# First batch of a fused attention and feed-forward kernel: load pieces dealt over both hardware queues, sines of k moved to ScalarE, transposed-q copies issued later

## The chip, the cores and the metric

One core of one Trainium2 chip. The metric is the device time in microseconds (us) of one execution. A run here is one such execution; each comparison has several, taken on the same chip as runs of the kernel before. The profile is of one execution, and its span (344.9 us for the kernel before) is about 1.8 us shorter than the time of the same execution.

## The reference

Cosformer attention (linear attention with position weights), then a gated feed-forward block. Batch 8, 8 heads, 576 positions, head dimension 64; model width 512, inner width 1536.

```python
theta = pi / 2 * arange(S) / S
phi(x) = concat([max(x, 0) * cos(theta), max(x, 0) * sin(theta)])   # 64 -> 128 features
kv  = einsum('bhsf,bhsd->bhfd', phi(k), v);   z = sum_s phi(k)
num = phi(q) @ kv;   den = phi(q) . z + 1e-6
x   = num / den                               # to [4608, 512], heads side by side
out = (gelu(x @ w_gate) * (x @ w_val)) @ w_out
```

## The kernel before

The kernel is one hand-ordered stream per engine. Nearly all of its time is the feed-forward matmuls, which cannot start before the first 256 rows of `x` exist. The path to them, the head of the kernel, is what the change touches. In batch 0:

- q, k and v arrive in pieces by pairs of heads (`m` counts four pairs).
- VectorE or ScalarE forms the cosine and sine halves of phi in bf16 (`prep_wide` on VectorE, `prep_act` on ScalarE; "sines" below are the sine halves of k that `prep_act` makes); v is cast to bf16.
- TensorE transposes phi(q) into PSUM; ScalarE and VectorE copy it out (`turn_q_pe`).
- Dummy matmuls (`keep_warm`) bridge the wait; they are meant to have TensorE at its full clock when real work comes. In the profile of this kernel each of them takes 311 ns up to about 11.4 us and 219 ns from then on. That moment is called the release of the clock.
- `kv_unit(0, 2)` multiplies phi(k) by v in two groups of two pairs, with a ScalarE copy after each group. `nm_unit` then makes numerators and denominators, `xt_unit` the transposed `x`, and `gv_unit` the first gate and value matmuls.

```python
load(nc.sync, "qf", q, 0, ((0, 2), (2, 2)), 0, 4)       # pieces (first pair, pairs), rows j 0..4
load(nc.scalar, "kf", k, 0, ((0, 2), (2, 2)))
load(nc.sync, "vf", v, 0, ((0, 2), (2, 1), (3, 1)))
load(nc.sync, "qf", q, 0, ((0, NP),), 4, R)
# ... constants; sin and cos tables on ScalarE; Gelu table load ...

for m in range(NP):
    for part in range(2):
        prep_wide("qp", 0, 0, 4, m, part)               # VectorE, 8 scalings of q
prep_act("kp", 0, 1, 0, 2)                              # ScalarE, 9 sines of k, pairs 0-1
turn_q_pe(0, 0, 4, (0, 1))                              # PE transposes, then copies at once
prep_wide("kp", 0, 0, R, 0, 0)
prep_wide("kp", 0, 0, R, 1, 0)
for m in (2, 3):
    for part in range(2):
        prep_wide("kp", 0, 0, R, m, part)               # VectorE, cosines AND sines of pairs 2-3
cast_v(0, 0, 2, nc.scalar.copy)
cast_v(0, 2, 1, nc.vector.tensor_copy)
cast_v(0, 3, 1, nc.vector.tensor_copy)
keep_warm(60)
kv_unit(0, 2)
nm_unit(0, 0)
nm_unit(0, 1, 0)
keep_warm(8)
xt_unit(0, 0)
# ...

def kv_unit(b, groups=1):
    # ... PSUM view psv, result tile kv ...
    for g in range(groups):
        # ... 36 matmuls of two pairs (72 of four, if groups is 1) ...
        nc.scalar.copy(kv[:, g * per:(g + 1) * per], psv[:, g * per:(g + 1) * per])
```

## Time and profile before

| | before |
|---|---|
| median of 3 runs | 346.81 us (346.61 to 347.16) |
| span of the profiled execution | 344.9 us |
| first kv matmul | 13.40 us |
| first num/den matmul | 15.98 us |
| first gate matmul | 19.80 us |

From the page of the kernel before: busy time of each engine, and TensorE's busy tenths in 40 slices of 8.6 us. (PE is TensorE, PEld its weight loads, DVE VectorE, ACT ScalarE, POOL GpSimd.)

```profile
PE 324.1 (94%) x2702; PEld 180.5 (52%) x2740; DVE 193.3 (56%) x534; ACT 138.0 (40%) x273; POOL 30.2 (9%) x51
PE   2889998989899999999999999999999999999994
```

TensorE is close to full in every slice but the first two or three and the last. So the head is where a change to batch 0 can gain: at most some of the 19.8 us.

The chain of waits of the kernel before, in order of time (start us, length us, what):

```profile
1.26 5.49 DMA qf<-in_q_dram
6.77 1.44 DVE qp L153 x4
...
8.87 4.60 PE psum L403 x60
13.47 0.71 PE psum L243 x36
...
14.20 0.39 ACT kv_sb L250
...
15.98 0.43 PE psum L259 x8
```

L403 is keep-warm, L243 kv, L250 the copy of kv, L259 num/den. The second q piece holds VectorE until 6.77 us; 60 keep-warm matmuls run to 13.47; the kv matmuls of pairs 2-3 wait for the copy of pairs 0-1.

Some lines of the timeline of the same stretch (start us, length us, engine, line, operation, output<-input, shapes, count, and in brackets the idle time before it and what ended it):

```profile
5.55 2.73 ACT L167 ACTIVATE kp<-kf,sin_t 128x128 bf16<-128x128 f32 x9 [0.54 <-DMA kf<-in_k_dram]
8.91 0.42 DVE L209 COPY qT_178<-psum 128x512 bf16<-128x512 bf16 x1 [0.70 <-PE psum L202]
9.22 1.16 ACT L175 CAST vx_119<-vf 128x1152 bf16<-128x1152 f32 x1
9.58 2.09 DVE L153 SCALAR_TENSOR_TENSOR kp<-kf,cos_t 128x576 bf16<-128x576 f32 x3
13.59 1.41 DVE L175 CAST vx_119<-vf 128x576 bf16<-128x576 f32 x2
14.62 0.89 PE L243 MATMUL psum<-vx_119,kp 64*128 64x65 bf16 x36 [0.47 <-ACT kv_sb L250]
```

VectorE is the busy one: from 8.91 to 15.00 us it has no gap, and its last v cast is the last input of pairs 2-3. ScalarE is idle from 10.4 to 14.2 us. That idle time is what the change wants to use.

### The profile page before, as it was taken

Reading aid. Unit: us, or ns where it says so; the run is one execution under the profiler, and the core shown is the slowest. Engines: PE = TensorE matmul, PEld = TensorE weight load, DVE = VectorE, ACT = ScalarE, POOL = GpSimd, SP = SyncE. Lnnn points to the kernel's source line nnn. Section 1 sums busy time; section 2 is a strip of 40 time slices with the busy share of each in tenths; the row PEclk is TensorE's granted clock in tenths of the full one; section 3 lists DMA queues with packets and bytes.
Section 4 is the critical chain, followed back from the end, with each engine's and each line's share of the span. In section 5 each row is a group of like instructions: output and inputs, shape, how many; then the busy total and the mean of one; then the engine's idle time right before and its main releaser. Section 6 shows DMA issues by size and latency. Waiting matters only on the chain.

```text
span 344.9 us, 6823 instructions
## 1 busy us (share of the span) xinstructions
PE 324.1 (94%) x2702; PEld 180.5 (52%) x2740; DVE 193.3 (56%) x534; ACT 138.0 (40%) x273; POOL 30.2 (9%) x51
## 2 busy tenths in 40 slices
PE   2889998989899999999999999999999999999994
PEld 1878757755445554555455545554555444444443
DVE  3777765993792598258825883588345222322300
ACT  7257965533433343334323433343244333223221
POOL 1831022000200200020002000110000000000000
PEclk9999999999999999999999999999999999999999
DMA  7999985019659907990789079606811111211124
GB/s 278 263 272 303 244 276 185 2 30 357 226 76 212 349 6 102 227 343 3 98 190 381 6 86 208 244 0 79 153 30 33 30 30 36 52 36 30 32 61 92
DMA packets 47889, 48.81 MB, mean 142 GB/s; under 512 B 25201, under 2 KB 33137, under 8 KB 47857
## 3 DMA queue, kind: packets, MB, share of 16 engines
q1 hardware_dynamic: 38672, 35.27, 40.3%
q0 software_dynamic: 8480, 11.80, 14.4%
q10 hardware_dynamic: 704, 1.31, 1.1%
q8 instruction: 21, 0.34, 0.4%
q14 instruction: 12, 0.09, 0.1%
HBM read 37.75 MB, written 9.44 MB: 137 GB/s over the span
## 4 chain that ended last, share of the span: by engine, by line
PE 89%; DVE 5%; DMA 2%; ACT 2%; issue 1%; SPq 0%; DVEq 0%; ACTq 0%
PE psum L321 52%; PE psum L352 25%; PE psum L243 3%; PE psum L259 3%; PE psum L299 2%; DMA qf<-in_q_dram 2%; PE psum L202 1%; PE psum L403 1%; DVE kp L143 1%; DVE x_sb L272 1%; DVE hT L332 1%; PE psum L564 1%; ACT xT L306 0%; DVE qp L153 0%; ACT gel L329 0%
## 5 line engine op out<-in xcount | busy, mean ns | idle before, releaser
L332 DVE TENSOR_TENSOR hT<-gel,psum 128x512 bf16<-128x512 f32 (+4 forms) x132 | 77.5, 589 | 126.8 <-PE psum L321 115.1
L329 ACT ACTIVATE gel<-psum 128x512 f32<-128x512 f32 (+4 forms) x132 | 68.6, 520 | 127.6 <-PE psum L321 121.5
L321 PE MATMUL psum<-xT,wg_sb 128*128 128x512 bf16 (+4 forms) x515 | 113.6, 339 | 2.4 <-ACT xT L306 1.4
L321 PE MATMUL psum<-xT,wv_sb 128*128 128x512 bf16 (+4 forms) x516 | 113.1, 339 | 0.6
L352 PE MATMUL psum<-wo_sb,hT 128*128 128x512 bf16 x407 | 104.3, 379 | 1.2 <-issue 0.8
L321 PEld LDWEIGHTS <-wg_sb 128*128 128x128 bf16 x528 | 48.4, 98 | 47.2 <-issue 2.1
L321 PEld LDWEIGHTS <-wv_sb 128*128 128x128 bf16 x528 | 49.0, 98 | 45.4
L352 PEld LDWEIGHTS <-hT 128*128 128x128 bf16 x420 | 38.7, 98 | 39.0
L306 ACT COPY xT<-psum 128x512 bf16<-128x512 bf16 (+1 forms) x44 | 22.0, 509 | 24.4 <-PE psum L299 24.3
L361 ACT COPY o_sb<-psum 128x512 f32<-128x512 f32 x35 | 20.5, 586 | 27.7 <-PE psum L352 26.3
L272 DVE TENSOR_TENSOR x_sb<-psum,rec 128x512 bf16<-128x512 f32 x40 | 27.7, 691 | 1.4
L143 DVE TENSOR_SCALAR qp<-qf,cos_t 128x256 bf16<-128x256 f32 x68 | 24.0, 353 | 0.0
L143 DVE TENSOR_SCALAR kp<-kf,cos_t 128x256 bf16<-128x256 f32 x63 | 21.6, 347 | 0.0
L143 DVE TENSOR_SCALAR qp<-qf,sin_t 128x256 bf16<-128x256 f32 x59 | 20.4, 346 | 0.0
L143 DVE TENSOR_SCALAR kp<-kf,sin_t 128x256 bf16<-128x256 f32 x57 | 19.8, 347 | 0.0
L299 PE MATMUL psum<-ident,x_sb 128*128 128x128 bf16 x160 | 15.5, 219 | 1.7 <-DVE x_sb L272 1.5
L202 PE MATMUL psum<-ident,qp 128*128 128x128 bf16 x108 | 9.2, 232 | 7.4 <-DVE qp L153 6.3
L175 POOL CAST vx_121<-vf 128x576 bf16<-128x576 f32 x12 | 7.5, 672 | 96.3 <-DMA vf<-in_v_dram 96.3
L175 POOL CAST vx_119<-vf 128x576 bf16<-128x576 f32 (+1 forms) x10 | 7.3, 767 | 65.3 <-DMA vf<-in_v_dram 65.3
L243 PEld LDWEIGHTS <-kp 64*128 64x128 bf16 x576 | 10.1, 94 | 4.8 <-issue 2.6
L299 PEld LDWEIGHTS <-x_sb 128*128 128x128 bf16 x160 | 10.1, 97 | 4.7 <-DVE x_sb L272 3.5
L202 PEld LDWEIGHTS <-qp 128*128 128x128 bf16 x108 | 7.3, 103 | 9.4 <-DVE qp L153 7.2
(90 smaller groups left out, 161.1 us busy)
## 6 DMA issues: line engine op xcount, KB each, us to landing
out_dram<-o_sb SPq DMA_DIRECT2D x70, 128.0 KB, 2.4
qf<-in_q_dram SPq DMA_DIRECT2D x5, 1152.0 KB, 11.6
kf<-in_k_dram SPq DMA_DIRECT2D x5, 1152.0 KB, 6.0
vf<-in_v_dram SPq DMA_DIRECT2D x5, 1152.0 KB, 9.2
qf<-in_q_dram POOLq DMA_DIRECT2D x2, 1152.0 KB, 16.3
kf<-in_k_dram POOLq DMA_DIRECT2D x2, 1152.0 KB, 11.5
vf<-in_v_dram POOLq DMA_DIRECT2D x2, 1152.0 KB, 11.7
wo_sb<-in_moe_w_out_dram POOLq DMA_DIRECT2D x2, 768.0 KB, 17.8
```

Source lines behind the costliest of these rows:

```text
L143: nc.vector.tensor_scalar(dst[:, m:m + n, j, part * D:(part + 1) * D], src[:, m:m + n, j], 0.0, (cos_t, sin_t)[part][:, j:j + 1], op0=ALU.max,
L175: copy(vx_tiles[b % 2][:, m:m + n, :, 0:D], staged["vf", b][:, m:m + n].rearrange("p m (j d) -> p m j d", j=R),)
L202: nc.tensor.transpose(out=views[m // per][:, m % per, j], in_=phi["qp", b][:, m, j0 + j, :], identity=ident,)
L243: nc.tensor.matmul(psv[:, pair, i], lhsT=kp[rr, pair, j, :], rhs=vx[rr, pair, j, :], start=(j == 0), stop=(j == R - 1),)
L272: nc.vector.tensor_tensor(x, nm[:, :, :, 0:D], rec[:, :, :, None].to_broadcast([128, 2, 4, D]), op=ALU.mult,)
L299: nc.tensor.transpose(out=ps[:, ct, :], in_=x[:, ct * 128:(ct + 1) * 128], identity=ident)
L306: nc.scalar.copy(xT_block(blk)[:, :, c:c + m], ps[:, :, o:o + m])
L321: nc.tensor.matmul(ps[:, 0:n], lhsT=w[:, ct, js], rhs=xt[:, ct, cc:cc + n], start=(ct == 0), stop=(ct == CT - 1),)
L329: nc.scalar.activation(gel[:, 0:n], g_ps[:, 0:n], AF.Gelu)
L332: nc.vector.tensor_mul(hT[blk][:, jt, cc:cc + n], gel[:, 0:n], v_ps[:, 0:n])
L352: nc.tensor.matmul(o_ps[i], lhsT=hT[blk][:, jt, tt * 128:(tt + 1) * 128], rhs=wo_sb[:, jt, :], start=(jt == 0), stop=(jt == JT - 1),)
L361: nc.scalar.copy(o_sb, o_ps.pop(i))
```

## The change

Intent: let q arrive first on both queues, so that VectorE does all q scalings in one run; give the sines of pairs 2-3 to ScalarE; take the v cast of pairs 0-1 in exchange; put the copies of transposed q last, since num/den needs them only after kv. The loads of v pair 3 and of the rest of q go to ScalarE's queue. Keep-warm goes from 60 to 50, with 8 more after kv.

```diff
-    load(nc.sync, "qf", q, 0, ((0, 2), (2, 2)), 0, 4)
-    load(nc.scalar, "kf", k, 0, ((0, 2), (2, 2)))
-    load(nc.sync, "vf", v, 0, ((0, 2), (2, 1), (3, 1)))
-    load(nc.sync, "qf", q, 0, ((0, NP),), 4, R)
+    load(nc.sync, "qf", q, 0, ((0, 2),), 0, 4)
+    load(nc.scalar, "qf", q, 0, ((2, 2),), 0, 4)
+    load(nc.sync, "kf", k, 0, ((0, 2),))
+    load(nc.scalar, "kf", k, 0, ((2, 2),))
+    load(nc.sync, "vf", v, 0, ((0, 2),))
+    load(nc.sync, "vf", v, 0, ((2, 1),))
 ...  (after the sine and cosine tables on ScalarE)
+    load(nc.scalar, "vf", v, 0, ((3, 1),))
+    load(nc.scalar, "qf", q, 0, ((0, NP),), 4, R)
 ...  (turn_q_pe split: the transposes, and turn_copies for the copies)
+    turn_q_pe(0, 0, 4, (0, 1), (None, None))
     prep_act("kp", 0, 1, 0, 2)
-    turn_q_pe(0, 0, 4, (0, 1))
     prep_wide("kp", 0, 0, R, 0, 0)
     prep_wide("kp", 0, 0, R, 1, 0)
-    for m in (2, 3):
-        for part in range(2):
-            prep_wide("kp", 0, 0, R, m, part)
-    cast_v(0, 0, 2, nc.scalar.copy)
+    cast_v(0, 0, 2, nc.vector.tensor_copy)
+    prep_act("kp", 0, 1, 2, 2)
+    prep_wide("kp", 0, 0, R, 2, 0)
+    prep_wide("kp", 0, 0, R, 3, 0)
     cast_v(0, 2, 1, nc.vector.tensor_copy)
     cast_v(0, 3, 1, nc.vector.tensor_copy)
+    turn_copies(0, 0, 4, (0, 1), (nc.scalar.copy, nc.vector.tensor_copy))
 ...
-    keep_warm(60)
+    keep_warm(50)
     kv_unit(0, 2)
+    keep_warm(8)
     nm_unit(0, 0)
```

More of the change, by code (lines that the diff above doesn't have):

```diff
@@ L206, in turn_q_pe, with turn_copies @@
                 )
-        for g, copy in zip(range(len(banks)), engines):
+        if engines[0] is not None:
+            turn_copies(b, j0, n, banks, engines)
+    def turn_copies(b, j0, n, banks, engines):
+        per = NP // len(banks)
+        for g, copy in enumerate(engines):
+            ps = psum[:, banks[g]].bitcast(BF16)[:, 0:per * n * 128].rearrange(
+                "f (m j c) -> f m j c", m=per, j=n
+            )
             for i in range(2):
@@ L212, in turn_q_pe @@
                     ].rearrange("f m (j p) -> f m j p", p=64),
-                    views[g][:, :, :, i * 64:(i + 1) * 64],
+                    ps[:, :, :, i * 64:(i + 1) * 64],
                 )
```

## The prediction

> **What bounds the kernel now.** The busy table gives PE 94% of a 344.9 us span; the 40-slice row shows PE at 8-9 tenths everywhere after the first slice. From 19.80 us on (first gate matmul) PE is dense and nothing changes. What can be won is the head. The chain of waits reads there: q load to 6.77 us; four q scalings (1.44); transposes; 60 keep-warm matmuls, 8.87 to 13.47; kv matmuls of pairs 0-1; ScalarE copy; kv matmuls of pairs 2-3, 14.62 to 15.53; copy; first num/den matmul at 15.98; then 3.8 us (divide, transpose, xT copy) to 19.80. By the timeline, VectorE works without a break from 8.91 to 15.00: qT copies (0.75), six k scalings (0.67 apart), then the v casts that release pairs 2-3. So VectorE and the keep-warm run bind together.
>
> **What the change does.** Loads: the second q piece lands at 6.77 now, behind 2304-byte k packets of the other queue. I estimate the q pieces at 3.8 and 4.9, k at 6.5 and 7.8 (was 5.55 and 8.7), v of pairs 0-1 at 9.5 (about 9.0 now), from packet rates in the trace. The Trainium skill, "DMA: Bandwidth & Descriptors", section "Issuing engines are not separate DMA queues", says queues share the same 16 engines and only interleave. The trace agrees: both queues together move 391 to 396 GB/s from 4 to 10 us; order changes, not rate.
>
> VectorE: all q scalings in one run, 3.8 to 6.5 (ended 8.2). It loses two k scalings (2 x 0.67) to ScalarE and gains the 1152-column v cast (about 1.27). The qT copies move to last. The sum hardly changes; it starts earlier but, I expect, sits 1.5 us waiting for v after two k scalings (8.0 to 9.5). Then cast to 10.8, k to 12.1, casts to 13.5, qT copies to 14.25.
>
> ScalarE: 18 sines at 0.30: 6.6 to 12.0 (was 9 from 5.55), qT copies to 13.0, then the first kv copy; it loses the 1.16 us cast. Two DMA issues (1.1 us) push the Gelu table load, hidden behind k.
>
> PE: transposes end near 7.0 instead of 8.87; 50 keep-warm matmuls end near 11.5. "TensorE: Matmul & The Clock Gate", Part 1, makes the warm-up a time (about 3.4 us of activity), not a count; in the trace keep-warm durations fall from 311 to 219 ns at about 11.3 us. So fewer, earlier matmuls may run mostly cold. Kv of pairs 0-1 at 11.5, of pairs 2-3 at 13.45 to 14.3, copy to 14.7, num/den at 14.8.
>
> **On the path.** About 1.2 us of 15.98 is gained, and carried whole through the 3.8 us and the dense remainder, since weights are issued earlier too (their gate, the second k piece, lands 0.9 us sooner).
>
> **Prediction:** 345.6 us, 344.4 to 346.6. Faster by over 2%: 0.01; within 2%: 0.98; slower: 0.01.
>
> **What would show it.** First q scaling before 4.2 and last ending before 7; VectorE idle 1 to 2 us before the large v cast, released by the v load; first sine at 6.2 to 7; first num/den at 14.3 to 15.3; first gate matmul at 18.1 to 19.1; the interval from there to the end unchanged within 0.3 us.
>
> **What would make it wrong.** v landing near 8.5 would add up to 1 us of gain. v at 10.5, or sines plus qT copies holding the first kv copy beyond 13.5, would eat the gain; so would a clock still throttled at 12 us, or later stages re-absorbing the head start in a load wait.

## The result, and the profile after

| | before | after |
|---|---|---|
| median of 4 runs | 346.99 us (346.61 to 347.25) | 345.87 us (345.63 to 346.18) |
| span of the profiled execution | 344.9 | 344.4 |
| first num/den matmul | 15.98 | 15.47 |
| first gate matmul | 19.80 | 19.29 |
| from there to the end of the span | 325.1 | 325.1 |

The ratio is 0.9969, with a 95% interval of 0.9952 to 0.9987: a gain of 0.3%, real but within the 2% that counts as the same. A ratio is the mean time of one kernel's runs over that of the other's of the same rounds, so it is not quite the ratio of the medians. The profiles are 0.5 us apart and the medians 1.1, because a profile is of one execution: that of before took 346.72 us, less than its median, and that of the changed kernel 346.18, the slowest of its four. The changed kernel was profiled once more below: its gate matmul then came at 19.09.

The chain of waits of the changed kernel, which answers to that of before:

```profile
1.75 8.46 DMA vf<-in_v_dram
...
10.23 1.04 DVE vx_119 L180
11.27 1.32 DVE kp L158 x2
12.59 1.32 DVE vx_119 L180 x2
13.92 0.34 DVE qT_194 L222
14.26 0.75 PE psum L256 x36
...
```

Here L158 is VectorE's scalings, L172 the sines, L180 the v casts, L222 the copies of transposed q, L417 keep-warm, L256 kv and L263 the copy of kv.

Taken at its word, the chain says that the v load now binds, and behind it VectorE, down to its copy of transposed q. But the kv matmuls of pairs 2-3 (L256) don't read transposed q. Some lines of the timeline show another candidate:

```profile
4.34 0.42 DVE L158 SCALAR_TENSOR_TENSOR qp<-qf,cos_t 128x256 bf16<-128x256 f32 x1 [2.75 <-DMA qf<-in_q_dram]
7.57 4.88 PE L417 MATMUL psum<-ident 128*128 128x128 bf16 x50
7.60 5.38 ACT L172 ACTIVATE kp<-kf,sin_t 128x128 bf16<-128x128 f32 x18 [2.59 <-DMA kf<-in_k_dram]
10.23 1.04 DVE L180 CAST vx_119<-vf 128x1152 bf16<-128x1152 f32 x1 [1.26 <-DMA vf<-in_v_dram]
12.51 1.40 DVE L180 CAST vx_119<-vf 128x576 bf16<-128x576 f32 x2
12.88 0.57 ACT L222 COPY qT_194<-psum 128x512 bf16<-128x512 bf16 x1
13.35 0.58 ACT L222 COPY qT_195<-psum 128x512 bf16<-128x512 bf16 x1
13.82 0.37 ACT L263 CAST kv_sb<-psum 128x260 bf16<-128x260 f32 x1
13.84 0.41 DVE L222 COPY qT_194<-psum 128x512 bf16<-128x512 bf16 x1
14.25 0.75 PE L256 MATMUL psum<-vx_119,kp 64*128 64x65 bf16 x36 [1.11 <-DVE qT_194 L222]
```

ScalarE, half idle before, now works from 7.60 to 14.19 us without a gap: 18 sines, two q copies, and only then the copy of kv of pairs 0-1, which had been ready since 13.13 (12.38 plus 0.75). That copy ends at 14.19; the first VectorE q copy ends at 14.25; the matmuls start at 14.25. Two ends 0.06 us apart: the profile infers the releaser, and cannot be trusted between them.

### The profile page after: what moved, and what is told of

It reads as the page before. It is cut to its first block, busy times and chain, and to the rows that moved or that the text cites. A ratio compares the mean times of both kernels' runs of the same rounds, so it can differ in the third digit from the quotient of the medians.

```text
span 344.4 us, 6826 instructions
## 1 busy us (share of the span) xinstructions
PE 324.5 (94%) x2700; PEld 180.9 (53%) x2738; DVE 192.4 (56%) x533; ACT 139.3 (40%) x281; POOL 30.5 (9%) x51
## 4 chain that ended last, share of the span: by engine, by line
PE 88%; DVE 6%; DMA 2%; ACT 1%; issue 1%; SPq 0%; DVEq 0%; ACTq 0%
PE psum L334 52%; PE psum L365 25%; PE psum L256 3%; PE psum L272 3%; PE psum L312 2%; DMA vf<-in_v_dram 2%; DVE kp L148 1%; PE psum L207 1%; DVE x_sb L285 1%; DVE hT L345 1%; PE psum L579 1%; DVE vx_119 L180 1%; ACT xT L319 0%; DVE kp L158 0%; ACT gel L342 0%
## 5 line engine op out<-in xcount | busy, mean ns | idle before, releaser
L180 POOL CAST vx_121<-vf 128x576 bf16<-128x576 f32 x12 | 7.5, 669 | 96.0 <-DMA vf<-in_v_dram 65.1
L180 POOL CAST vx_119<-vf 128x576 bf16<-128x576 f32 (+1 forms) x10 | 7.2, 765 | 65.6 <-DMA vf<-in_v_dram 65.6
L256 PEld LDWEIGHTS <-kp 64*128 64x128 bf16 x576 | 10.1, 95 | 5.4 <-issue 3.4
## 6 DMA issues: line engine op xcount, KB each, us to landing
qf<-in_q_dram SPq DMA_DIRECT2D x5, 1152.0 KB, 11.6
kf<-in_k_dram POOLq DMA_DIRECT2D x2, 1152.0 KB, 11.4
vf<-in_v_dram POOLq DMA_DIRECT2D x2, 1152.0 KB, 11.8
```

The lines of the kernel that those rows point to most:

```text
L180: copy(vx_tiles[b % 2][:, m:m + n, :, 0:D], staged["vf", b][:, m:m + n].rearrange("p m (j d) -> p m j d", j=R),)
L256: nc.tensor.matmul(psv[:, pair, i], lhsT=kp[rr, pair, j, :], rhs=vx[rr, pair, j, :], start=(j == 0), stop=(j == R - 1),)
```

## The experiments

Two theories of what binds the head of the changed kernel:

- **A, ScalarE.** The first kv copy stands behind 18 sines and two q copies in ScalarE's queue, and it releases pairs 2-3.
- **B, the v load and VectorE**, as the chain of waits says.

And a question of the change itself: is it the load order or the compute order that gains? Each kernel got five to six runs, with 11 runs of the kernel before in the same set of four; all gave correct results. The three sets (rows 2 to 5, 6 to 9 and 10 to 13) ran on three different chips, so a difference between medians of two sets may hold a difference of the chips; the ratio, which is to runs of the kernel before on the same chip, is the safer figure. "First gate" is the first gate matmul in the kernel's profile.

| kernel | median us | ratio to before (95%) | first gate us |
|---|---|---|---|
| before, three sets | 346.92, 346.84, 347.10 | | 19.80 |
| changed, again | 345.91 | 0.9972 (0.9960 to 0.9985) | 19.09 |
| loads only | 345.75 | 0.9964 (0.9951 to 0.9977) | 18.98 |
| compute order only | 345.72 | 0.9973 (0.9955 to 0.9990) | 18.55 |
| changed, kv copy first | 345.19 | 0.9952 (0.9940 to 0.9964) | 18.28 |
| changed, k scalings before v cast | 346.04 | 0.9973 (0.9959 to 0.9986) | 19.18 |
| changed, 9 wide sines | 345.68 | 0.9960 (0.9948 to 0.9973) | 19.02 |
| before, 50 keep-warm | 346.68 | 0.9989 (0.9976 to 1.0002) | 19.86 |
| changed, three edits | 345.50 | 0.9955 (0.9942 to 0.9968) | 18.43 |
| changed, kv in one group | 345.46 | 0.9955 (0.9942 to 0.9968) | 18.39 |
| changed, k by single pairs | 345.27 | 0.9948 (0.9936 to 0.9960) | 18.61 |
| old loads, one group | 345.33 | 0.9950 (0.9935 to 0.9964) | 18.12 |
| new loads, one group | 344.43 | 0.9925 (0.9913 to 0.9938) | 17.52 |

In every one of these profiles the span less the time of the first gate matmul is 325.0 to 325.4 us. So whatever is gained or lost in the head goes whole into the span, and the first gate matmul can be read in place of the span.

### The changed kernel again (no edit)

> The changed kernel once more, unedited, as the control of this set: ratio to the kernel before 0.9955 to 0.9985, the first num/den matmul at 15.3 to 15.6 us and the first gate matmul at 19.1 to 19.4 us, as in its first profile (15.47 and 19.29; before 15.98 and 19.80). If the gain of 1.1 us by the medians is typical and the profiled 0.5 us was an unlucky execution, the first gate matmul is nearer 18.9.

It held, to within 0.03 us: 345.91 us and ratio 0.9972, first gate at 19.09 (19.1 or later expected), first num/den at 15.27 (15.3 or later). In this execution VectorE ended its casts sooner, and the profile names ScalarE for the same wait that it put down to VectorE before:

```profile
13.57 0.74 DVE L222 COPY qT<-psum 128x512 bf16<-128x512 bf16 x2
13.62 0.37 ACT L263 CAST kv_sb<-psum 128x260 bf16<-128x260 f32 x1
14.05 0.75 PE L256 MATMUL psum<-vx,kp 64*128 64x65 bf16 x36 [0.90 <-ACT kv_sb L263]
```

### The kv copy ahead of the q copies

```diff
-    turn_copies(0, 0, 4, (0, 1), (nc.scalar.copy, nc.vector.tensor_copy))
 ...
-    kv_unit(0, 2)
+    kv_unit(0, 2, lambda: turn_copies(   # called in kv_unit, after the copy of group 0
+        0, 0, 4, (0, 1), (nc.scalar.copy, nc.vector.tensor_copy)
+    ))
```

> The changed kernel with the four q copies issued after the first kv copy instead of before it. Theory A (ScalarE binds: 18 sines to 12.98, two q copies to 13.9, then the first kv copy, which releases the kv matmuls of pairs 2-3 at 14.25): these start at 13.5 to 13.6, the first num/den matmul at about 14.95 instead of 15.47, 0.5 us faster than the changed kernel. Theory B (what the chain of waits says: the v load at 10.23 and VectorE's casts and q copies behind it): pairs 2-3 still start at 14.2 or later, under 0.15 us gained.

It gained 0.7 us over the changed kernel (means of the five runs each, of the same set: 345.31 and 346.02), as theory A said (the intervals of the two ratios just overlap), and pairs 2-3 started at 12.96, sooner than expected. The timeline:

```profile
7.63 3.53 PE L418 MATMUL psum<-ident 128*128 128x128 bf16 x50
...
12.07 1.40 DVE L180 CAST vx<-vf 128x576 bf16<-128x576 f32 x2
12.52 0.35 ACT L263 CAST kv_sb<-psum 128x260 bf16<-128x260 f32 x1
...
12.96 1.03 PE L256 MATMUL psum<-vx,kp 64*128 64x65 bf16 x36 [1.11 <-ACT kv_sb L263]
```

The copy comes right behind the sines, and the matmuls of pairs 2-3 start as it ends. They now take 1.03 us instead of 0.75, as pair 3 waits for its v cast (13.47): VectorE is next in line.

A part of what this profile shows is the clock and not the edit. Its keep-warm run (L418) took 3.53 us, against 4.88 and 4.67 in the two profiles of the changed kernel, because the clock was released at 8.9 us and not at 11.4 to 11.6; so kv of pairs 0-1 was done at 11.84. Had keep-warm ended near 12.4, as it did there, that kv would have ended near 13.15 and the copy could not have begun at 12.52. An estimate from these numbers puts pairs 2-3 at about 13.6 then, 0.5 to 0.7 us sooner than in the two profiles of the changed kernel, instead of 1.1 to 1.3. The times say that the gain is not this luck alone: the mean granted clock differs among the five runs (1.000, 0.997, 0.997, 1.000, 0.998), and the first four of them, 345.14 to 345.30 us, lie below all nine runs of the unedited changed kernel (345.63 to 346.61).

### The k scalings ahead of the v cast

```diff
-    cast_v(0, 0, 2, nc.vector.tensor_copy)
     prep_act("kp", 0, 1, 2, 2)
     prep_wide("kp", 0, 0, R, 2, 0)
     prep_wide("kp", 0, 0, R, 3, 0)
+    cast_v(0, 0, 2, nc.vector.tensor_copy)
```

> The changed kernel with VectorE's k scalings of pairs 2-3 moved ahead of the large v cast, into the 1.26 us in which it waited for v. Theory B (v load and VectorE bind): VectorE's last v cast ends near 12.7 instead of 13.91 and the first num/den matmul comes 0.8 to 1.2 us earlier. Theory A (ScalarE binds): VectorE does end earlier, but the first kv copy still starts at 13.8, kv of pairs 2-3 at 14.2 to 14.3, gain under 0.15 us.

VectorE did end its casts 1.05 us sooner than in the changed kernel's first profile (12.86 against 13.91), and no gain is seen: 346.04 us, ratio 0.9973. The timeline:

```profile
11.44 1.42 DVE L180 CAST vx<-vf 128x576 bf16<-128x576 f32 x2 [0.46 <-DMA vf<-in_v_dram]
12.77 0.75 DVE L222 COPY qT<-psum 128x512 bf16<-128x512 bf16 x2
13.72 0.37 ACT L263 CAST kv_sb<-psum 128x260 bf16<-128x260 f32 x1
14.14 0.76 PE L256 MATMUL psum<-vx,kp 64*128 64x65 bf16 x36 [0.80 <-ACT kv_sb L263]
```

VectorE's casts and q copies were all done at 13.52, and pairs 2-3 still waited for ScalarE until 14.14. The clock does not blur this reading: kv of pairs 0-1 was done at 13.34, and the copy began only at 13.72, behind ScalarE's q copies. Theory B falls as the first limit. These two runs decide between A and B.

### The parts of the change alone

Loads only is the kernel before with the new load lines and nothing else of the change. Compute order only is the changed kernel with the four old load lines.

```diff
# loads only, against before           # compute order only, against the changed kernel
-    (four old load lines)              -    (eight new load lines)
+    (eight new load lines)             +    (four old load lines)
```

> The kernel before with only the new order of loads. If the gain comes from q landing earlier (my prediction's reading): VectorE's q scalings end near 7.1 us, its six k scalings near 12.3, v casts near 13.7, 60 keep-warm matmuls end near 12.9, the first num/den matmul at about 15.35, gain about 0.6 us, that is nearly all of the whole change's gain in the trace. If the load order gains nothing by itself and the compute order does the work: first num/den at 15.8 to 16.0.

> The changed kernel with the old load order (k first on the second queue, v and the q rest behind q on the first). Worked out from durations: sines done near 11.4, q copies on ScalarE near 12.5, 50 keep-warm matmuls end near 12.75, kv of pairs 0-1 to 13.5, its copy to 13.9, pairs 2-3 from 13.95, first num/den at about 15.1: a gain of about 0.9 us, more than the whole change has in its trace (0.5), because v lands at 9.2 and the sines start at 5.55. If the load order is what gains (my prediction), this stays at 15.8 or later.

The first num/den matmul came at 15.16 us with the loads only (about 15.35 expected) and at 14.73 with the compute order only (about 15.1 expected, and 15.8 or later if the load order were what gains). So each half gains by itself, and the reading that only the load order does is refuted.

Each half by itself gives about what both give together: 345.75 and 345.72 us, against 345.91 for the whole. The intervals overlap, so none of the three is shown faster than another. The profiles say where each half leads. Loads only:

```profile
7.25 2.74 ACT L172 ACTIVATE kp<-kf,sin_t 128x128 bf16<-128x128 f32 x9 [2.24 <-DMA kf<-in_k_dram]
...
13.51 0.38 ACT L255 CAST kv_sb<-psum 128x260 bf16<-128x260 f32 x1 [1.52 <-PE psum L248]
```

Compute order only:

```profile
5.40 2.74 ACT L167 ACTIVATE kp<-kf,sin_t 128x128 bf16<-128x128 f32 x9 [0.39 <-DMA kf<-in_k_dram]
...
13.08 0.38 ACT L258 CAST kv_sb<-psum 128x260 bf16<-128x260 f32 x1 [0.88 <-PE psum L251]
```

In both, ScalarE sits idle before its first kv copy (1.52 and 0.88 us) and TensorE's keep-warm run sets the time (in their chains of waits it runs from 7.85 to 12.79 us and from 8.73 to 12.36). With both halves together ScalarE has the longer list and gets its first input two microseconds later than with the old loads: the sines start at 7.4 to 7.6 instead of 5.4, and the copy slips to 13.6 to 13.8. So the halves don't add. Of its six runs, compute order only had two at 346.8 and 347.1 us and four at 345.4 to 345.8; why is not settled. The length of the keep-warm run (below) is a suspect: the mean granted clock is 0.999 in both of the slower runs and 0.997 in each of the four others. This mean also holds a fall of the clock near the end of a run (to half at 341.5 us in the profile of compute order only), so it tells that the clock changed at other moments, not by how much the release was late.

### k dealt by single pairs

```diff
-    load(nc.sync, "kf", k, 0, ((0, 2),))
-    load(nc.scalar, "kf", k, 0, ((2, 2),))
+    load(nc.sync, "kf", k, 0, ((0, 1), (2, 1)))
+    load(nc.scalar, "kf", k, 0, ((1, 1), (3, 1)))
```

> The changed kernel with k dealt by single pairs: pairs 0 and 2 on the first queue, 1 and 3 on the second. Now pairs 0-1 and 2-3 run side by side on the two queues and land at about 7.4 and 8.1 us. If this interleaving is why k of pairs 0-1 lands 1.9 us later than in the kernel before (5.55), pairs 0-1 now land at 6.3 to 6.7, the sines start about 0.9 us sooner and end near 12.0, the first kv copy starts near 13.0, and the gain over the changed kernel is 0.2 to 0.5 us (then VectorE's v casts bind). If the later landing has another cause (a slow engine of the sixteen): sines start at 7.2 or later, no gain.

This asks why k of pairs 0-1 lands so late in the changed kernel. With pairs 0 and 1 both at the head of their queues, these land at 5.62 and 5.99 us by the trace, and the sines start at 6.74 and even there wait for the Gelu table, not for k:

```profile
6.63 0.20 ACT L127 ACTIVATE warm<-half_pi 128x1 f32<-128x1 f32 x1
6.74 5.35 ACT L172 ACTIVATE kp<-kf,sin_t 128x128 bf16<-128x128 f32 x18
```

The table load began at 5.34 us here instead of 3.51, behind ScalarE's last two load issues (4.49 and 4.86), so not all of the earlier k is used. It gains: 345.27 us, ratio 0.9948, against the 0.9972 of the changed kernel in another set; in its profile the kv matmuls behind the keep-warm run end at 13.09 and ScalarE's q copies at 13.04, so that both now hold the first kv copy (13.13). So the deal by halves was the cause of the late landing, and a slow engine of the sixteen is not needed to explain it: in the changed kernel the two pieces of k, of equal size, are under way side by side on the two queues, and the one needed first landed only shortly before the other (7.51 and 8.03 us; 7.32 and 8.38 in the second profile). Within each queue the pieces landed in the order of issue in these profiles, but a piece shares its time with whatever runs beside it.

### Nine wide sines

```diff
-    prep_act("kp", 0, 1, 0, 2)
+    prep_act("kp", 0, 1, 0, NP)
 ...
-    prep_act("kp", 0, 1, 2, 2)
```

> The changed kernel with the 18 sines of two pairs each (128x128) replaced by 9 of four pairs each (128x256, 0.50 us each, about 0.41 apart). They need both k pieces, so start at 8.1 instead of 7.6, and end near 11.8 instead of 12.98. Theory A: q copies to 12.9, first kv copy at about 13.15, pairs 2-3 from 13.5 with pair 3 waiting for the v cast at 13.91, first num/den at about 14.75, 0.7 us faster than the changed kernel. Theory B: no gain over 0.15 us.

The nine sines took 3.70 us, as expected, but began half a microsecond late, with the second k piece (8.56 to 12.26 us instead of 8.1 to 11.8), and ScalarE was idle 0.35 us before the first kv copy. The gain is small where 0.7 us was expected (345.68 us, ratio 0.9960, the interval overlapping that of the changed kernel), and the chain of waits of its profile shows why:

```profile
8.13 4.69 PE psum L416 x50
...
13.55 0.38 ACT kv_sb L263
```

The 50 keep-warm matmuls ran to 12.82 and became the limit. The expectation had left them out.

### The kernel before with 50 keep-warm matmuls

```diff
-    keep_warm(60)
+    keep_warm(50)
```

> The kernel before with 50 keep-warm matmuls instead of 60. My prediction said that the keep-warm run and VectorE bind together. If so, taking 10 away alone lets kv of pairs 0-1 start 0.55 us sooner (12.9) but pairs 2-3 still wait for the v casts (14.34 and 15.0): first num/den at 15.85 to 16.0, gain 0 to 0.1 us. If keep-warm alone bound it: gain about 0.5 us.

Inconclusive for the question, and instructive. The median is 0.16 us lower, and the interval of the ratio (0.9976 to 1.0002) allows no gain as well as one of 0.8 us. But in the profiled execution the 50 matmuls took longer than the 60 before (4.95 us in the chain, against 4.60):

```profile
8.72 4.95 PE psum L403 x50
```

In the profile of compute order only, 50 of them from almost the same start took 3.63 us:

```profile
8.73 3.63 PE psum L412 x50
```

There the duration of one fell from 314 to 219 ns at 10.4 us, here only at 13.2. So the number of matmuls alone doesn't set the length of this run; when the clock is released does too.

### Three edits together

Wide sines, k scalings ahead of the v cast, and `keep_warm(40)` on the changed kernel.

> The changed kernel with the nine wide sines, the k scalings of pairs 2-3 ahead of the v cast, and 40 keep-warm matmuls instead of 50. Theory A with B next in line: sines to 11.8, q copies to 12.9, keep-warm to about 11.4, kv of pairs 0-1 to 12.6, its copy 12.9 to 13.3, pairs 2-3 to 14.1, first num/den at about 14.5, about 1 us faster than the changed kernel and 1.5 to 2 us faster than the kernel before. If fewer keep-warm matmuls let the clock stay low, the matmuls after 11.4 us show 311 ns instead of 219.

345.50 us, about 0.4 below the changed kernel by the medians of two sets, less than the 1 us expected. The first gate matmul is at 18.43: ScalarE's sines ended at 12.12, but the two q copies still stood ahead of the kv copy (12.96), and pairs 2-3 waited for it until 13.39. Of the clock: the keep-warm matmuls fell to 219 ns at 11.3 us, before their end at 11.82, so 40 of them were enough in this execution. The kv matmuls of pairs 0-1 took 0.92 us instead of 0.75 for another reason:

```profile
11.75 0.92 PE L256 MATMUL psum<-vx,kp 64*128 64x65 bf16 x36
```

In the trace sixteen of them start between 11.75 and 11.99 us and the next only at 12.17, just after the last wide sine ended (12.12). Each takes 189 to 202 ns, before that gap and after it. They waited for a sine, not for the clock.

### kv in one group

```diff
-    kv_unit(0, 2)
+    kv_unit(0)
```

> The changed kernel with the kv product of batch 0 in one group: all 72 matmuls, then one copy of 520 columns, instead of two halves with a copy each. Reason: in every trace the matmuls of pairs 2-3 wait for the copy of pairs 0-1, though they write other columns. If that wait is what makes the first kv copy (and so ScalarE's sines and q copies ahead of it) count: kv of pairs 2-3 run when their v casts are done (13.2 and 13.6 to 13.9), end at about 14.2, the copy to 14.9, first num/den at about 14.95: 0.3 to 0.5 us faster than the changed kernel. If the wait costs nothing by itself: no gain, or a loss of 0.2 us from the larger copy.

345.46 us, first num/den at 14.56 instead of 15.27 to 15.47. Part of that is luck of this execution, in which k and v landed 0.3 us sooner; by the medians of two sets the gain over the changed kernel is 0.45 us, with intervals that overlap. The matmuls of pair 2 start at 12.76, right behind their v cast, with no copy made yet:

```profile
12.76 0.47 PE L256 MATMUL psum<-vx,kp 64*128 64x65 bf16 x18 [0.44 <-DVE vx L180]
13.92 0.59 ACT L263 CAST kv_sb<-psum 128x520 bf16<-128x520 f32 x1 [0.47 <-PE psum L256]
```

So the wait of pairs 2-3 for the copy of pairs 0-1 was no need of the data. One copy of 520 columns takes 0.59 us; two of 260 took 0.75 and the wait.

### Two versions meant to beat both

Old loads, one group: the changed compute order with the old load lines, `keep_warm(40)`, and

```diff
-    cast_v(0, 2, 1, nc.vector.tensor_copy)
-    cast_v(0, 3, 1, nc.vector.tensor_copy)
+    cast_v(0, 2, 2, nc.vector.tensor_copy)
-    kv_unit(0, 2)
+    kv_unit(0)
```

New loads, one group: the same two edits and `keep_warm(40)` on the changed kernel, with the wide sines and the k scalings ahead of the v cast.

> A version meant to beat both: the changed compute order with the old load order, kv in one group, v of pairs 2-3 cast by one 128x1152 instruction, 40 keep-warm matmuls. The large cast took 0.77 to 1.04 us where two of 576 columns took 1.41, so VectorE gains about 0.5 us. Expected: sines done near 11.4, casts near 12.2, keep-warm near 12.0 (clock phase permitting, 11.5 to 12.7), kv to 13.5, copy to 14.1, first num/den at about 14.2, first gate matmul near 18.0, 344.9 us, 0.9 us faster than the changed kernel.

> The same with the new load order, nine wide sines and the k scalings of pairs 2-3 ahead of the v cast: sines to 12.1 and q copies to 13.1, casts to 12.4 to 12.9, keep-warm to 11.8, kv to 13.3 to 13.6, copy to 14.2, first num/den at about 14.25, first gate matmul near 18.1. If both load orders come out within 0.2 us of each other, the order of loads does not matter once ScalarE's queue and the copy between the groups are off the path.

New loads, one group is the fastest of all: 344.43 us, ratio 0.9925 (0.9913 to 0.9938), some 2.7 us below the kernel before of its set and 1.5 us below the changed kernel of another set; its first gate matmul came at 17.52 us, 0.6 us sooner than expected. Its interval touches only those of the next two (old loads, one group, and k by single pairs), and its five runs, 344.29 to 345.03 us, lie below all five of the latter (345.21 to 345.52). With the old loads the median is 0.9 us higher (345.33, where 344.9 was expected), over a wide spread (344.74 to 346.02 us in six runs). So the condition, both within 0.2 us, was not met, and the new loads seem to be the better ones once ScalarE is off the path; the two versions also differ in their sines and in the place of the v cast, so it isn't isolated. In the profiles the keep-warm run starts after the last transpose of q, at 7.85 us against 8.91 in the chains, and ends at 11.71 against 12.35. The timeline of the fastest:

```profile
7.64 4.07 PE L415 MATMUL psum<-ident 128*128 128x128 bf16 x40
...
11.29 0.76 DVE L180 CAST vx<-vf 128x1152 bf16<-128x1152 f32 x1 [0.46 <-DMA vf<-in_v_dram]
11.65 1.36 PE L256 MATMUL psum<-vx,kp 64*128 64x65 bf16 x72
13.05 0.59 ACT L263 CAST kv_sb<-psum 128x520 bf16<-128x520 f32 x1 [0.22 <-PE psum L256]
```

Engines now end within a microsecond of each other, and 72 kv matmuls run without a break. It was not tried with k dealt by single pairs.

## Why the prediction was right or wrong

The time was right: 345.6 us predicted, 345.87 measured (though the range, 344.4 to 346.6 us, would have held almost no gain as well), and the gain was of the expected kind (a head start of about a microsecond, carried whole to the end). Of its steps, some held and some only cancelled out.

- **Only the head changes, and the rest carries it whole.** Right: the interval from the first gate matmul to the end is 325.1 us in both profiles.
- **q lands first and is scaled in one run.** Right in kind, but half a microsecond later than predicted: 4.34 to 7.11 us instead of 3.8 to 6.5, so that both of its marks (first scaling before 4.2, last ending before 7) were missed.
- **VectorE idle 1 to 2 us before the large v cast, released by the v load.** Right: 1.26 us. v landed at 10.2 instead of 9.5. Mis-sized the other way was the cast itself, 1.27 us expected, 1.04 measured, and 0.77 to 0.86 us in most later profiles.
- **k at 6.5 and 7.8.** This term was mis-sized and is the one that mattered: the first k piece landed at 7.5 (7.3 in the second profile). It ran beside the other k piece of the same size and landed only 0.5 to 1.1 us ahead of it; dealt by single pairs, k of pairs 0-1 was there by 5.99. So the first sine was at 7.60 and not at 6.2 to 7, the 18 sines ended at 12.98 instead of 12.0, and the first kv copy began at 13.82 instead of 13.0.
- **What binds pairs 2-3.** The prediction named both, VectorE's cast and the kv copy, and listed "sines plus qT copies holding the first kv copy beyond 13.5" as what would eat the gain. That happened. Moving the kv copy ahead gave 0.7 us; relieving VectorE gave nothing.
- **Two DMA issues push the Gelu table load.** Wrong and harmless: the table load began at 3.51 us in both profiles, as the two issues (1.89 to 2.84 us) ran beside the table load before it.
- **Keep-warm ends near 11.5.** Wrong in the profile, 12.38: most of the 50 ran at 314 ns. It was harmless there, as ScalarE was later, and became the limit once the sines were shortened.
- **"VectorE and the keep-warm run bind together" in the kernel before.** Not refuted and not shown: 10 fewer keep-warm matmuls lowered the median by 0.16 us, with an interval from no gain to 0.8 us, and the late release of the clock spoilt the profile.
- **First num/den at 14.3 to 15.3, first gate at 18.1 to 19.1.** Missed by 0.2 us in the first profile, inside in the second (15.27, 19.09). The profiled gains (0.5 and 0.7 us) fall short of the predicted 1.2, by about the 0.8 us that the kv copy came late. The medians give 1.1, because the execution profiled for before was 0.27 us faster than its median (346.72 against 346.99) and that of the changed kernel 0.31 us slower (346.18 against 345.87). So the close agreement of the total is partly luck.

## What to carry to other kernels

When work is moved to an idle engine, look at what that engine does next that others wait for: here a 0.37 us copy stood behind 6 us of sines and q copies, and putting it ahead of the q copies was worth some 0.5 to 0.7 us where the whole change brought 1.1. Where loads run side by side on two queues, as here, deal the pieces so that those needed first run side by side with each other, not with those needed later. When two candidate releasers end within 0.1 us of each other, don't believe the profile's choice; speed up each one alone and see which moves the wait. And before a profile is read for the worth of an edit, look at when the clock was released in it: in the profiles here that moment lay anywhere from 8.9 to 13.2 us.

## What the Trainium skill lacked or had wrong

- "DMA: Bandwidth & Descriptors", section "Issuing engines are not separate DMA queues", says that issuing from several engines only saves issue time, as transfers interleave. This case agrees on rate (393 GB/s before, from 4 to 6 us), but the order of use is worth time that the section doesn't mention: the new load lines alone, with the same bytes, took the median from 346.92 to 345.75 us, and dealing k by single pairs brought the first sine to 6.74 us, from 7.1 to 7.6 in the other profiles with the new loads and sines of two pairs.
- "TensorE: Matmul & The Clock Gate", Part 1, says that the moment of warm-up varies by about 0.5 us either way. Here it varied more: with the dummy matmuls beginning at 8.5 us behind the same transposes in two profiles, their durations fell from 314 to 219 ns at 10.4 us in one and at 13.2 us in the other, 2.8 us apart, so that 50 of them took 3.63 us and 4.95. Counted from TensorE's first transpose (the transposes leave gaps), the fall came 3.6 to 7.6 us later over all profiles, where the prediction reckoned with about 3.4 us of activity. For a kernel head tuned to tenths that is no small term.
- "ScalarE: Activation LUTs", section "What ACT_TABLE_LOAD costs", puts a change of tables at 1283 ns and about 1380 ns of drain. The loads took 1.28 us here, but no drain is to be seen: the activation before one load ends at 3.50 us, the load begins at 3.51 and the next activation at 4.81. Its formula for one ACTIVATE (186 ns, 0.833 ns a column, 93 ns for a pointer operand) fits: 386 and 492 ns by it, 388 and 494 ns measured for 128 and 256 columns.
- "VectorE: DVE Perf Modes", section "What auto-detection actually checks", asks for outermost dimensions that are both even or equal for the double rate. The casts fit that reading, though no run here isolates the mode: two casts of 128x576, which the trace lists with one run of 576 as source and 9 rows of 64 as target (even and odd), took 0.74 us apiece, while those of 128x1152, with 1152 and 18 rows (both even), took 0.75 to 0.86 for twice the columns. One such cast took 1.04 us, in the first profile of the changed kernel. It began 0.03 us after its source had landed, but others that began as soon after took 0.77 to 0.82, so that is not the reason; it stays open.
- No page warns that a profile's inferred releaser can be the wrong one of two that end 0.06 us apart (14.19 and 14.25 us here).
